# Two paddings in SBUF that move the stationary operands of the float32r matmuls

## The chip, the core and the metric

One core of one Trainium2 chip runs the whole kernel. The metric is the device time of one execution in microseconds; the median of several runs is given. The names of the engines are those of the profile: PE is TensorE, PEld its weight loads, DVE VectorE, ACT ScalarE, POOL GpSimd, SP SyncE, which issues nearly all DMAs.

## The reference

A transformer block over S = 2048 tokens of width D = 448, with 16 heads of 28 columns, and an MLP whose hidden width is split into two halves of FH = 896. Everything is float32.

```python
mod = (silu(c) @ w_mod).reshape(1, 6, 1, -1)          # sa, ca, ga, sb, cb, gb
h = layernorm(x) * (1 + ca) + sa
q, k, v = split(h @ wqkv)                              # 16 heads
o = softmax(q @ k.T * 28 ** -0.5) @ v
x = x + ga * (o @ wo)
h = layernorm(x) * (1 + cb) + sb
z = gelu(h @ w_in)
z1, z2 = z[..., :896], layernorm(z[..., 896:])
g = w_sp @ z2 + b_sp[:, None]                          # mixes the tokens, 2048 x 2048
x = x + gb * ((z1 * g) @ w_out)
```

## The kernel before

**Precision.** Most matmuls are in float32r, and each float32 operand is split into a high and a low part, both float32r. A product then takes several matmuls (high x high, low x high, high x low) that accumulate in PSUM. Where the contraction is over 448 rows, the list STEPS (11 pairs of a slice of the activations and a slice of the weights) says which parts meet. P·V and the transposes are in plain float32.

**Operands.** In `pe.matmul(out, a, b)`, `a` is the stationary operand, which a weight load puts into the array, at most 128 columns of 4 bytes, that is 512 bytes of each partition; `b` is the moving operand, 448 or 512 columns here. The profile names the moving operand first or last without meaning; what is stationary is told below.

**Memory.** Three pools last long: `const` at the low end of SBUF, `dpool` at the high end (side "right") with one big tile heapD, and pools that come and go between them. heapD is reused all through by views: hT (the normalised activations) and wqk (the weights of q and k), then OT (the output of attention) and wos, then w2 and half of z2, then uT. After attention three more big tiles come at the low end: heapA (w1, then part of z2), heapB (h2T, then the rest of z2 and the high part of w_out) and heapC (the last group of h2T, then the low part of w_out). Every view's slices are multiples of 448 or 512 elements apart, so all stationary slices taken from one big tile have the same first byte modulo 512.

**Stages, in order.**
- 0 to about 115 us: modulation vectors, layernorm, `ln_transpose`, `v_tile` (stationary hT in heapD, moving wv, L241) and `qk_unit` (stationary wqk, moving hT, both heapD, L249). The results of qk_unit go to DRAM (qk_scr) as a high and a low part.
- about 115 to 905 us: attention. For each head `load_head` brings k and q to `kst` and `qst`, three tiles of each in turn, in the pool `stk`. `m_mm` (L346: stationary qst, moving kst, 84 rows) makes scores whose row maxima DVE takes (L351, TENSOR_REDUCE); `m_fin` writes the negated maxima into two more rows of qst. `s_mm` (L377: stationary kst, moving qst, 86 rows) makes the scores less their maxima, of which ACT takes the exponential into P (L381). `pv_mm` (L392: stationary V, moving P, float32) follows for two units of 128 keys at a time. The order is written out by hand in the loop over `u` (256 units): four s_mm and four m_mm alternate, m_mm LEAD = 20 units ahead, and after each second unit 16 records of P·V. So a pair of units is a burst of 16 matmuls and then P·V. The PSUM tiles of both kinds come from one ring of seven. The last 20 units have s_mm alone.
- about 905 to 1010 us: `wo_mm` (stationary OT, moving wos, both heapD, L561), the second layernorm, `z1_unit` (stationary w1 in heapA, moving h2T in heapB or heapC, L672).
- to about 1097 us: `z2_gemm` (stationary h2T in heapB or heapC, moving w2 in heapD, L744) and `z2_norm`, which puts z2[0..7] in heapD, z2[8..11] in heapA and z2[12..15] in heapB.
- to the end: the mixing of tokens. For each block `tb` of 512 tokens, `mix_part(tb, st, f)` (L792, L793, L794: stationary z2[st], moving the high and low parts of the weights in `wsp`) runs over 16 values of st and 7 of f. `gate` forms u, split into uT (heapD), and `y_part` (stationary uT, moving w_out in heapB and heapC, L832 to L834) of one block is spread through the mixing of the next.

Tiles in a pool are laid out in the order in which they are asked for, so a tile that nothing uses moves those that come after it, and one in a pool on the right side moves all that lies below it.

Of the kernel before, what the change touches and what calls it, by code (L numbers as in the profile page):

```python
# [8 lines left out]
F32 = mybir.dt.float32  # L9
# [24 lines left out]
def tile_adaln_mha_gmlp(ctx, tc, x, wqkv, wo, w_in, w_spT, b_sp, w_out, cT, w_mod, out):  # L34
# [5 lines left out]
    dpool = ctx.enter_context(tc.tile_pool(name="dpool", bufs=1, side="right"))  # L40
# [17 lines left out]
        cols[nm] = const.tile([128, 4], F32, name=f"col_{nm}")  # L58
    bcs = {"gb": const.tile([128, D], F32, name="bc_gb")}

    heapD = dpool.tile([128, 24 * 896], F32R, name="heapD")

    def hview(heap, off, a, b):
        return heap[:, off : off + a * b].rearrange("p (a b) -> p a b", b=b)
# [254 lines left out]

    stk = att.enter_context(tc.tile_pool(name="stk", bufs=1))  # L320
    ppool = att.enter_context(tc.tile_pool(name="ppool", bufs=6))
    kst = [stk.tile([128, S], F32R, name=f"kst{i}") for i in range(3)]
    qst = [stk.tile([128, S], F32R, name=f"qst{i}") for i in range(3)]
    npool = att.enter_context(tc.tile_pool(name="npool", bufs=2))
# [584 lines left out]
```

## Time and profile before

| | |
|---|---|
| median of 3 runs | 1481.84 us (1479.3 to 1483.68) |
| the profiled execution | 1484.28 us |
| its span, first to last instruction | 1482.5 us |
| mean granted TensorE clock | 0.994 |
| DVE busy | 60% |
| ACT busy | 49% |
| POOL busy | 20% |

In a group's row, the tiles are out<-in, then rows x columns; after the first bar stand busy time in us and the mean duration of one in ns, after the second the idle time of the engine before them. Matmuls overlap in the pipeline, so a duration is longer than the distance between two starts; that distance is read from the first column of the timeline. A row of the timeline with x6 merges six neighbours: start of the first, time from there to the end of the last.

The first bytes of the stationary operands modulo 512, from the built program:

| stationary | lines | before |
|---|---|---|
| heapD: hT, wqk, OT, z2[0..7], uT | 241, 249, 561, 792 to 794, 832 to 834 | 480 |
| kst, qst | 346, 377 | 320 |
| heapA, heapB, heapC: w1, h2T, z2[8..15] | 672, 744, 792 to 794 | 64 |

### The profile page before, as it was taken

To read this page: it belongs to the slowest core of one execution; us is meant where nothing else is said; L and a number is where in the kernel's file an instruction comes from. 1 tells how busy PE (TensorE), PEld (TensorE's weight loads), DVE (VectorE), ACT (ScalarE), POOL (GpSimd) and SP (SyncE) were. 2 spreads that over 40 slices of the span, in tenths; PEclk is the share of its full clock that TensorE was granted. 3 is DMA by queue.
4 is the path that set the end of the run, shared out by engine and by line. 5 is a ranking of instruction groups with operands and counts; after the bars stand their busy time and mean duration, and the time that the engine had idled before them with its cause. 6 is when DMAs were issued, how large, how long until landed. Compare 5 with 4: busy or idle time off the path is not lost. (4 is left out here: it accounts for less than half of the span.)

```text
span 1482.5 us, 19584 instructions
## 1 busy us (share of the span) xinstructions
PE 1444.3 (97%) x7284; PEld 1014.8 (68%) x7284; DVE 891.8 (60%) x1469; ACT 723.7 (49%) x1374; POOL 294.2 (20%) x282
## 2 busy tenths in 40 slices
PE   4998999999999999999999999999999999999999
PEld 3886755555555555555555547778988888888887
DVE  6726888888888888888888821752541411413114
ACT  3522467677677676776776784343432210211111
POOL 4723300000002011101000021540763300302002
PEclk8999999999999999999999999999999999999999
DMA  9336402210122112221022004632003322323223
GB/s 233 107 108 203 151 17 52 52 41 25 40 52 52 39 35 57 52 48 43 16 51 52 12 20 122 206 111 100 8 21 102 114 75 68 106 62 101 84 68 106
DMA packets 58790, 111.57 MB, mean 75 GB/s; under 512 B 12006, under 2 KB 27462, under 8 KB 56006
## 3 DMA queue, kind: packets, MB, share of 16 engines
q1 hardware_dynamic: 58534, 109.40, 25.9%
q8 instruction: 57, 0.93, 0.3%
q0 software_dynamic: 160, 0.92, 0.2%
q14 instruction: 39, 0.32, 0.1%
HBM read 76.15 MB, written 29.49 MB: 71 GB/s over the span
## 5 line engine op out<-in xcount | busy, mean ns | idle before, releaser
L351 DVE TENSOR_REDUCE pm<-mt 128x1 f32<-128x512 f32 x1024 | 628.1, 682 | 131.0 <-PE mt L346 129.8
L381 ACT ACTIVATE P<-st_ps 128x512 f32<-128x512 f32 x1024 | 514.2, 620 | 153.7 <-PE st_ps L377 153.3
L377 PE MATMUL st_ps<-qst,kst 86*128 86x512 f32 x1024 | 409.8, 411 | 0.0
L346 PE MATMUL mt<-kst,qst 84*128 84x512 f32 x1024 | 400.7, 397 | 5.2 <-DMA qst<-qk_scr 3.2
L377 PEld LDWEIGHTS st_ps<-qst,kst 86*128 86x128 f32 x1024 | 192.8, 189 | 145.1 <-issue 80.5
L392 PE MATMUL o_ps<-P,V 128*32 128x512 f32 x2048 | 247.5, 598 | 0.0
L346 PEld LDWEIGHTS mt<-kst,qst 84*128 84x128 f32 x1024 | 194.6, 190 | 45.0 <-DVE pm L351 4.5
L70 DVE TENSOR_TENSOR wsp_l<-raw_sp,wsp_h 128x512 fp32r<-128x512 f32 x64 | 48.7, 763 | 193.0 <-ACT wsp_h L727 193.0
L727 ACT ACTIVATE wsp_h<-raw_sp 128x512 fp32r<-128x512 f32 x64 | 40.4, 631 | 248.6 <-DMA raw_sp<-in_w_spT_dram 170.9
L392 PEld LDWEIGHTS o_ps<-P,V 128*32 128x32 f32 x2048 | 54.1, 109 | 123.1 <-issue 116.2
L70 POOL TENSOR_TENSOR heapD<-u,heapD 128x512 fp32r<-128x512 f32 x27 | 44.6, 1685 | 261.2 <-ACT heapD L811 261.2
L418 POOL TENSOR_TENSOR osb<-osb,rb 128x512 f32<-128x512 f32 x16 | 20.4, 1277 | 366.3 <-DMA rb<-r_scr 220.7
L792 PE MATMUL acc<-wsp_h,heapD 128*128 128x512 f32 x224 | 89.2, 398 | 2.9 <-ACT zg L747 1.6
L794 PE MATMUL acc<-wsp_h,heapD 128*128 128x512 f32 x224 | 88.5, 395 | 0.0
L793 PE MATMUL acc<-wsp_l,heapD 128*128 128x512 f32 x224 | 88.3, 394 | 0.0
L249 PE MATMUL pq<-heapD 128*128 128x512 f32 x308 | 79.8, 398 | 0.0
L249 PEld LDWEIGHTS pq<-heapD 128*128 128x128 f32 x308 | 58.6, 191 | 13.6 <-issue 0.4
L70 POOL TENSOR_TENSOR nl<-nf,nh 16x128 fp32r<-16x128 f32 x16 | 7.2, 451 | 272.8 <-issue 180.6
L672 PE MATMUL z_ps<-heapB,heapA 128*128 128x512 f32 x231 | 54.5, 396 | 0.0
L744 PE MATMUL z_ps<-heapD,heapB 128*128 128x448 f32 x264 | 53.0, 363 | 0.0
L837 DVE TENSOR_TENSOR x2t<-x2t,y_ps 128x448 f32<-128x448 f32 x12 | 7.5, 621 | 75.7 <-PE y_ps L834 75.7
L744 PEld LDWEIGHTS z_ps<-heapD,heapB 128*128 128x128 f32 x264 | 49.6, 188 | 3.3
(156 smaller groups left out, 1629.0 us busy)
## 6 DMA issues: line engine op xcount, KB each, us to landing
raw_sp<-in_w_spT_dram SPq DMA_DIRECT2D x64, 256.0 KB
kst<-qk_scr SPq DMA_DIRECT2D x48, 224.0 KB
qst<-qk_scr SPq DMA_DIRECT2D x48, 224.0 KB
qk_scr<-qh SPq DMA_DIRECT2D x28, 256.0 KB
qk_scr<-ql SPq DMA_DIRECT2D x28, 256.0 KB
z_scr<-z1t SPq DMA_DIRECT2D x28, 256.0 KB
z<-z_scr SPq DMA_DIRECT2D x28, 256.0 KB
wm<-in_w_mod_dram SPq DMA_DIRECT2D x6, 784.0 KB
```

The source lines that it names most:

```text
L70: eng.tensor_tensor(out=dst, in0=a, in1=hi.bitcast(F32), op=ALU.subtract)
L249: pe.matmul(pq, wqk[:, b, m * 128 : (m + 1) * 128], hT[g][:, a, :], start=j == 0, stop=j == NST - 1)
L346: pe.matmul(mt, qst[h % 3][0:84, t * 128 : (t + 1) * 128], kst[h % 3][0:84, kb * 512 : (kb + 1) * 512], start=True, stop=True)
L351: dve.tensor_reduce(out=pms[h][:, t, kb : kb + 1], in_=mt, axis=AX.X, op=ALU.max)
L377: pe.matmul(st, kst[h % 3][0:86, kt * 128 : (kt + 1) * 128], qst[h % 3][0:86, qb * 512 : (qb + 1) * 512], start=True, stop=True)
L381: act.activation(p, st, AF.Exp, scale=SCALE)
L392: pe.matmul(otile[h][32 * qb : 32 * qb + 32, :], V[:, kt, h, :], ptiles.pop((u, qb)), start=kt == 0, stop=kt == NT - 1)
L672: pe.matmul(ps_t, w1[:, b, f * 128 : (f + 1) * 128], h2T[g][:, a, :], start=j == 0, stop=j == NST - 1)
L744: pe.matmul(ps_t[:, :D], h2T[g][:, a, tt * 128 : (tt + 1) * 128], w2[:, b, hf * D : (hf + 1) * D], start=j == 0, stop=j == NST - 1)
L792: pe.matmul(acc[f], z2[st][:, 0, fs], hi, start=st == 0, stop=False)
L793: pe.matmul(acc[f], z2[st][:, 0, fs], lo, start=False, stop=False)
L794: pe.matmul(acc[f], z2[st][:, 1, fs], hi, start=False, stop=st == NT - 1)
```

## The change

A tile of 104 float32 per partition is asked for behind heapD, in the pool on the right side, and one of 64 float32 ahead of kst and qst. Neither is read or written. heapD and what lies below it on the right side (the staging tiles of q, k and of the heads' outputs) move down by 416 bytes, so that heapD starts at 64 modulo 512; kst, qst and what follows them in `stk` and the pools after it (the P buffers, the small tiles of the maxima) move up by 256 bytes, so that kst and qst start at 64 modulo 512. heapA, heapB, heapC, V and wsp stay. The moving operands in the moved tiles move with them: wqk's partner hT, kst and qst, P, wos, and w2, whose first bytes go from 480 and 224 to 64 and 320.

```diff
@@ -58,7 +58,9 @@
         cols[nm] = const.tile([128, 4], F32, name=f"col_{nm}")
     bcs = {"gb": const.tile([128, D], F32, name="bc_gb")}
 
+
     heapD = dpool.tile([128, 24 * 896], F32R, name="heapD")
+    dpool.tile([128, 104], F32, name="padD")
 
     def hview(heap, off, a, b):
@@ -319,6 +321,7 @@
 
     stk = att.enter_context(tc.tile_pool(name="stk", bufs=1))
     ppool = att.enter_context(tc.tile_pool(name="ppool", bufs=6))
+    stk.tile([128, 64], F32, name="padS")
     kst = [stk.tile([128, S], F32R, name=f"kst{i}") for i in range(3)]
     qst = [stk.tile([128, S], F32R, name=f"qst{i}") for i in range(3)]
```

## The prediction, made before the run

> **What bounds the kernel now.** I read the page first, for the share of each engine by slice; then the groups of instructions with shapes kept apart, for the same matmul from different tiles; then the timeline, for the distance between neighbouring starts; last the built program's addresses, since the change moves nothing else.
>
> ```profile
> span 1482.5 us, 19584 instructions
> PE 1444.3 (97%) x7284; PEld 1014.8 (68%) x7284; DVE 891.8 (60%) x1469; ACT 723.7 (49%) x1374; POOL 294.2 (20%) x282
> ```
>
> TensorE is busy 97% of the span, so what counts is the distance from one matmul start to the next. The diff can act on nothing else: in the built program every instruction, operand shape and wait stands where it stood, on all five engines. Only addresses differ. heapD moves from byte 143328 to 142912 (480 to 64 modulo 512), kst and qst move up by 256 bytes (320 to 64), and with them the P buffers and the staging tiles. So no wait is added or moved past.
>
> The trace of before already holds the comparison. In the mixing stage `z2[st]` lies in heapD for st 0 to 7 (480), in heapA and heapB for st 8 to 15 (64); the moving `wsp` tiles are at 64 throughout, and code, stage and shapes are one. Groups, last figures before the second bar: busy us, mean ns of one:
>
> ```profile
> L792 PE MATMUL acc<-wsp_h,heapD 128*128 128x512 f32 x224 | 89.2, 398 | 2.9 <-ACT zg L747 1.6 <-DVE u L809 1.3
> L793 PE MATMUL acc<-wsp_l,heapD 128*128 128x512 f32 x224 | 88.3, 394 | 0.0
> L794 PE MATMUL acc<-wsp_h,heapD 128*128 128x512 f32 x224 | 88.5, 395 | 0.0
> L792 PE MATMUL acc<-wsp_h,heapA 128*128 128x512 f32 x112 | 43.6, 390 | 0.0
> L793 PE MATMUL acc<-wsp_l,heapB 128*128 128x512 f32 x112 | 43.6, 390 | 0.0
> L833 PE MATMUL y_ps<-heapB,heapD 128*128 128x448 f32 x98 | 36.1, 368 | 0.0
> L744 PE MATMUL z_ps<-heapD,heapC 128*128 128x448 f32 x88 | 17.8, 362 | 0.0
> ```
>
> The heapD groups average 396 ns, those from heapA and heapB 390. L744, 448 columns and a stationary at 64, takes 362 to 363; L833, 448 columns and a stationary in heapD, 368. The timeline (start, duration) says that this is real spacing and no matter of how an end is modelled:
>
> ```profile
> 1199.70 0.40 PE L792 MATMUL acc<-wsp_h,heapD 128*128 128x512 f32 x1
> ...
> 1201.10 0.40 PE L792 MATMUL acc<-wsp_h,heapD 128*128 128x512 f32 x1
> 1224.84 0.39 PE L792 MATMUL acc<-wsp_h,heapA 128*128 128x512 f32 x1
> ...
> 1226.20 0.39 PE L792 MATMUL acc<-wsp_h,heapA 128*128 128x512 f32 x1
> ```
>
> Each pair is six matmuls apart: 1.40 us, 233 ns each, from heapD; 1.36 us, 227 ns each, from heapA.
>
> The Trainium skill speaks against the change here: "TensorE: Matmul & The Clock Gate", on step 1 of what a matmul does, says that TensorE reads stationary and moving operands through two independent SBUF ports, so that a weight load takes nothing from the running matmul. By that rule no address could matter. The 233 against 227 ns with one moving operand disagrees with it.
>
> **The change part by part.** Where the stationary lies in heapD and TensorE sets the pace:
> 1. Mixing from heapD, 3 x 224 = 672 matmuls, whose operands become 64 and 64 as those from heapA are now: (396 - 390) x 672, with unrounded means 5.7 ns, gives 3.8 us. Waits there are 2.9 us of 270, so nearly all is path.
> 2. y_part, 336 matmuls of 448 columns: 368 or 367 down to 363, 4.8 ns each, 1.6 us. It runs between the mixing matmuls, on the path.
> 3. v_tile, 176: six in the timeline take 1.39 us where six of L744 take 1.36, 5 ns apart once last durations are taken off; 0.9 us, 0 if the first 100 us (TensorE idle in places) swallow it.
> 4. wo_mm, 176: spacing 202 to 207 ns against L744's 200, 2.5 ns at least, 0.4 us (1.2 at most).
> 5. qk_unit, 308: stationary and moving are both at 480. Six in a row, from 102.69 us, take 1.52 us with the last one's 0.39, or 226 ns apart: nothing to gain. Between attention's matmuls they run slower, for the reason under attention. 0.
> 6. z2_gemm, 352, stationary unmoved at 64; its moving operand goes from 480/224 to 64/320. Now exactly 200 ns. No row has 448 columns with both at 64/320. Bounds: 0, and the 2.5 to 6.7 ns by which wo_mm (both operands in heapD, equal offsets) exceeds 200, a loss of 0.9 to 2.3 us. I take 0, since every group with a stationary at 64 is at its floor whatever it streams.
>
> **Attention** (L346, L377: 2048 matmuls, mean spacing 234 ns) would be the largest prize: 7 ns x 1888 (16 in each of the 118 pairs of units that hold both kinds) is 13 us. I take 0. Its stationary sits at 320, and at 320 it already runs at the low spacing once the two kinds stop alternating:
>
> ```profile
> 599.29 0.40 PE L346 MATMUL mt<-kst,qst 84*128 84x512 f32 x1
> ...
> 600.71 0.40 PE L346 MATMUL mt<-kst,qst 84*128 84x512 f32 x1
> 889.42 2.10 PE L377 MATMUL st_ps<-qst,kst 86*128 86x512 f32 x8
> ```
>
> Alternating 84 and 86 rows: six starts in 1.42 us, 237 ns. In the tail, eight score matmuls alone: 2.10 less the first gap of 0.34 and the last duration of 0.39, over six, is 228 ns, and the last two gaps are 226 and 227. The weight load tells the same: 190 ns after a matmul with another row count (L346's row has 190), 187 to 188 after one with the same. So the row count breaks the rhythm there, not the address. The bound above 0: a burst of 16 between two P·V groups could shorten by some 100 ns. But the weight load of its 15th matmul waits for the fourth reduction (L351, every 598 ns in the burst): in some 3 bursts of 10 it starts 106 ns or less before its matmul, and there an earlier PE only waits longer. So 0.7 x 100 + 0.3 x 25 = 78 ns, times 118 = 9 us. VectorE is next: eight reductions need 4.8 of a pair's 5.8 us.
>
> Weight loads of P·V (V unmoved, P moving) and the transposes show no dependence on offset: 0, as are the staging tiles' DMAs, which land behind a busy TensorE.
>
> **Sum.** 3.8 + 1.6 + 0.9 + 0.4 = 6.7 us. The profiled execution took 1484.28 us (span 1482.5 and 1.8 outside): 1477.6. It stands 2.4 us above the median of 1481.84, so 1475.1 in terms of medians, which I forecast.
>
> **The rivals** (median terms).
> - Attention gains as well: the pad was put there on the view that 320 is as bad as 480, and 234 ns equals heapD's 233. For it speaks that equality; against it the tail. 6.7 + 9 = 15.7: 1466.1; with no wait for the reductions, 1462.
> - Only the difference between the two operands' offsets counts. qk_unit at 480/480 and 226 ns speaks for it, z2_gemm's 200 at two differences against. Then mixing still gains 3.8, y_part, v_tile and wo_mm nothing, z2_gemm loses up to 2.3: 1478.0 to 1480.3.
> - Nothing happens: heapD may be slow for its place (above byte 142900, the others below 126100) and not its offset. qk_unit's 226 ns from heapD speaks against. 1481.8. The Trainium skill, "SBUF — State Buffer", Operand start alignment, asks only that an operand start at a multiple of its element size, which both layouts satisfy; it speaks of legality and not speed, and no run here bears on it otherwise.
> - Slower: attention settles at a worse rhythm. L377 to L346 shows gaps of 240 within bursts. If 240 became the rule in place of 233.3, 6.7 x 1888 = 12.6 us less the gain of 6.7: 1487.7. It decides from 6.7 / 1888 = 3.5 ns a matmul. Against it: the offset that goes away, 320, and the new one have nothing in the trace that tells them apart.
>
> **How the numbers follow.** Forecast 0.46; attention too 0.20; difference only 0.14; nothing 0.08; slower 0.12. A measurement of this kernel tells 0.3%, 4.4 us, from no change. The forecast (6.7) lies beyond that, with some chance of falling short of it: faster 0.66, same 0.21, slower 0.13. The likeliest case alone spans 1473 to 1478. The range reaches from attention's gain at 1463 to 1485, leaving out the rest of the slower case.
>
> **What would show it.** Right: heapD groups of L792 to L794 at 390, y_part's at 363, L744 still 362 to 363, L346 still about 397 with spacing 234 in attention. Wrong: L744 up at 365 to 369 (difference rules); L346 and L377 spaced 227 (attention gains), with longer waits of the L377 weight loads for L351; heapD still at 396 (place rules).

## The result and the profile after

| | before | after |
|---|---|---|
| median | 1481.76 us (20 runs) | 1476.2 us (20 runs) |
| ratio | | 0.9968, 95% interval 0.9957 to 0.998 |
| a second series, medians | 1480.91 us (20 runs) | 1475.71 us (8 runs) |
| ratio | | 0.9967, 0.9956 to 0.9978 |
| the profiled execution | 1484.28 us, span 1482.5 | 1473.13 us, span 1471.4 |

In the first series one execution of each kernel took far longer than the rest (2026.81 and 2867.84 us); the ratios leave such executions out. The kernel is 5.6 us faster by the first medians and 5.2 by the second. The two profiled executions lie 11.1 us apart, so one must not put the whole of that down to the change; the table of stages below separates it.

The page after, engines' busy time and share of the span:

```profile
span 1471.4 us, 19584 instructions
PE 1439.4 (98%) x7284; PEld 1015.8 (69%) x7284; DVE 888.1 (60%) x1469; ACT 723.4 (49%) x1374; POOL 294.6 (20%) x282
```

TensorE still bounds the kernel. The lines of the changed file are 2 or 3 higher: L795 to L797 are mix_part, L835 to L837 y_part, L747 z2_gemm, L349 and L380 m_mm and s_mm. The groups of instructions after, shapes kept apart (after the first bar: busy us, mean ns):

```profile
L795 PE MATMUL acc<-wsp_h,heapD 128*128 128x512 f32 x224 | 87.8, 392 | 1.9 <-ACT zg L750 1.2 <-DVE u L812 0.7
L796 PE MATMUL acc<-wsp_l,heapD 128*128 128x512 f32 x224 | 87.4, 390 | 0.1
L797 PE MATMUL acc<-wsp_h,heapD 128*128 128x512 f32 x224 | 87.4, 390 | 0.0
L795 PE MATMUL acc<-wsp_h,heapA 128*128 128x512 f32 x112 | 43.7, 390 | 0.0
L835 PE MATMUL y_ps<-heapB,heapD 128*128 128x448 f32 x98 | 35.7, 365 | 0.0
L836 PE MATMUL y_ps<-heapB,heapD 128*128 128x448 f32 x98 | 36.0, 367 | 0.0
L747 PE MATMUL z_ps<-heapD,heapC 128*128 128x448 f32 x88 | 18.0, 366 | 0.0
L349 PE MATMUL mt<-kst,qst 84*128 84x512 f32 x1024 | 401.3, 397 | 5.5 <-DMA qst<-qk_scr 3.5 <-DVE pm L354 1.6 <-ACT P L384 0.3
```

The mixing matmuls from heapD fell from 394 to 398 ns to 390 to 392, where those from heapA were all along. y_part went from 367 or 368 to 364 to 367, and not to 363. z2_gemm, whose stationary did not move, went up from 362 to 366. m_mm is where it was, at 397. The timeline of the mixing says the same in spacing: six starts in 1.36 us, 227 ns each, with stationary operands from heapD.

```profile
1194.68 0.39 PE L795 MATMUL acc<-wsp_h,heapD 128*128 128x512 f32 x1
...
1196.04 0.39 PE L795 MATMUL acc<-wsp_h,heapD 128*128 128x512 f32 x1
```

From the start records of both traces I took, for each function, the mean distance from one matmul to the next, leaving out distances over 260 ns, which are waits:

| function (columns) | before, ns | after, ns | count | gain, us |
|---|---|---|---|---|
| mix_part, heapD (512) | 233.4 | 227.5 | 672 | 4.0 |
| y_part (448) | 205.2 | 202.4 | 335 | 0.9 |
| v_tile (448) | 205.9 | 202.6 | 176 | 0.6 |
| wo_mm (448) | 203.1 | 203.5 | 176 | -0.1 |
| z2_gemm (448) | 200.1 | 202.7 | 352 | -0.9 |
| qk_unit (512) | 230.4 | 229.6 | 308 | 0.2 |
| m_mm, s_mm in bursts (512) | 234.3 | 234.2 | 1968 | 0 to 0.2 |

The last row counts 1024 s_mm, with those of the tail, and 944 m_mm. Together that makes 4.7 us, close to the 5.2 and 5.6 of the medians. By stages, each counted from the first matmul of one function to the first of the next:

| stage, us | before | after | after, second series |
|---|---|---|---|
| v_tile to s_mm | 154.6 | 150.8 | 150.4 |
| s_mm to wo_mm (attention) | 728.0 | 728.1 | 728.1 |
| wo_mm to z1_unit | 42.0 | 41.9 | 41.6 |
| z1_unit to z2_gemm | 78.4 | 76.8 | 77.5 |
| z2_gemm to mix_part | 72.2 | 72.7 | 72.7 |
| mix_part to the end | 384.8 | 379.1 | 380.5 |

Attention did not move at all, z2_gemm's stage got longer, mixing shorter by 4.3 to 5.7 us. The first stage looks 4 us shorter, but that is mostly how executions differ: in the runs below it lasts between 150.4 and 154.5 us whatever heapD's offset (150.9 and 151.2 with heapD at 480, 154.5 in one with heapD at 64).

### The profile page after: what moved, and what is told of

Its sections match the earlier page's. It is cut to its first block, busy times and chain, and to the rows that moved or that the text cites. A ratio compares the mean times of both kernels' runs of the same rounds, so it can differ in the third digit from the quotient of the medians.

```text
span 1471.4 us, 19584 instructions
## 1 busy us (share of the span) xinstructions
PE 1439.4 (98%) x7284; PEld 1015.8 (69%) x7284; DVE 888.1 (60%) x1469; ACT 723.4 (49%) x1374; POOL 294.6 (20%) x282
## 5 line engine op out<-in xcount | busy, mean ns | idle before, releaser
L380 PE MATMUL st_ps<-qst,kst 86*128 86x512 f32 x1024 | 410.1, 411 | 0.0
L349 PE MATMUL mt<-kst,qst 84*128 84x512 f32 x1024 | 401.3, 397 | 5.5 <-DMA qst<-qk_scr 3.5
L380 PEld LDWEIGHTS st_ps<-qst,kst 86*128 86x128 f32 x1024 | 192.9, 189 | 144.8 <-issue 80.5
L349 PEld LDWEIGHTS mt<-kst,qst 84*128 84x128 f32 x1024 | 195.3, 191 | 45.6 <-DVE pm L354 4.5
L795 PE MATMUL acc<-wsp_h,heapD 128*128 128x512 f32 x224 | 87.8, 392 | 1.9 <-ACT zg L750 1.2
L797 PE MATMUL acc<-wsp_h,heapD 128*128 128x512 f32 x224 | 87.4, 390 | 0.0
L747 PE MATMUL z_ps<-heapD,heapB 128*128 128x448 f32 x264 | 53.7, 366 | 0.0
L747 PEld LDWEIGHTS z_ps<-heapD,heapB 128*128 128x128 f32 x264 | 49.7, 188 | 3.9
```

Source lines behind the costliest of these rows:

```text
L349: pe.matmul(mt, qst[h % 3][0:84, t * 128 : (t + 1) * 128], kst[h % 3][0:84, kb * 512 : (kb + 1) * 512], start=True, stop=True)
L380: pe.matmul(st, kst[h % 3][0:86, kt * 128 : (kt + 1) * 128], qst[h % 3][0:86, qb * 512 : (qb + 1) * 512], start=True, stop=True)
L747: pe.matmul(ps_t[:, :D], h2T[g][:, a, tt * 128 : (tt + 1) * 128], w2[:, b, hf * D : (hf + 1) * D], start=j == 0, stop=j == NST - 1)
L795: pe.matmul(acc[f], z2[st][:, 0, fs], hi, start=st == 0, stop=False)
L797: pe.matmul(acc[f], z2[st][:, 1, fs], hi, start=False, stop=st == NT - 1)
```

## The experiments

Two things were open. First, whether the stationary operand's own offset counts, as the change's words have it, or the difference between the moving operand's and the stationary's. z2_gemm's loss spoke for the second. Second, whether attention's 234 ns comes from its row counts. A difference below is always moving less stationary, modulo 256.

**Each padding alone.**

```diff
 # e1: the changed kernel
-    stk.tile([128, 64], F32, name="padS")
 # e2: the changed kernel
-    dpool.tile([128, 104], F32, name="padD")
```

> The change with padD alone; kst and qst stay at 320. Theory (attention's pace comes from its alternating row counts, 84 and 86, and heapD's offset is all that works): same as with both paddings, 4 to 6 us below the kernel before; mixing matmuls from heapD 390 to 392 ns, attention spaced 234 ns. Rival (kst and qst at 64 give part of the gain): 2 us or more slower than with both.

> The change with padS alone; heapD stays at 480. Theory: within 1.5 us of the kernel before, attention spaced 234 ns, mixing from heapD still 396 ns. Rival (kst and qst at 64 give part of the gain): 2 to 9 us below the kernel before, with attention's spacing under 234.

Measured: padD alone 1478.46 us against 1480.4 of the kernel before, ratio 0.9981 (0.9969 to 0.9994); padS alone 1482.07, ratio 1.001 (0.9998 to 1.0022). The time with padD alone came out less far below before than expected (1.9 us and not 4 to 6); its interval overlaps that of both paddings, so the times by themselves do not exclude the rival. The traces decide it. One group of mixing from heapD, first with padD alone, then with padS alone:

```profile
L796 PE MATMUL acc<-wsp_h,heapD 128*128 128x512 f32 x224 | 87.3, 390 | 0.0
```

```profile
L796 PE MATMUL acc<-wsp_h,heapD 128*128 128x512 f32 x224 | 88.9, 397 | 0.0
```

With padD alone the mixing from heapD is spaced 227.4 ns, y_part 202.4, z2_gemm 202.7 and attention takes 727.6 us, each as with both. With padS alone mixing stays at 233.3, z2_gemm at 200.1, and attention takes 727.4. kst and qst at 64 in place of 320 do nothing.

**The stationary stays at 480, the moving operand goes there.** This is the kernel before, without either padding, and with one in front of the mixing weights:

```diff
     wp = ctx.enter_context(tc.tile_pool(name="wp", bufs=2))
+    wp.tile([128, 104], F32, name="padW", bufs=1)
```

> The kernel before, with the moving tiles wsp of the mixing 416 bytes further on: from 64 to 480 modulo 512. heapD, and with it half of the stationary z2, stays at 480. Theory (the difference of moving and stationary counts, modulo 256): heapD's mixing now has difference 0 and goes from 233.4 to 227.5 ns; heapA and heapB get 416, which is 160 modulo 256, as z2_gemm before, and stay at 227; 4 us below the kernel before. Rival (the stationary's own offset counts, 480 is bad and 64 good): heapD stays at 233 and heapA, heapB at 227, the time within 1.5 us of before.

Measured: 1482.31 us, ratio 1.0008 (1.0 to 1.0017). The groups of this run:

```profile
L793 PE MATMUL acc<-wsp_h,heapD 128*128 128x512 f32 x224 | 87.6, 391 | 2.2 <-ACT zg L748 1.6 <-DVE u L810 0.6
L795 PE MATMUL acc<-wsp_h,heapD 128*128 128x512 f32 x224 | 87.2, 389 | 0.0
L793 PE MATMUL acc<-wsp_h,heapA 128*128 128x512 f32 x112 | 44.4, 396 | 0.0
L795 PE MATMUL acc<-wsp_h,heapB 128*128 128x512 f32 x112 | 44.4, 396 | 0.0
```

The two have changed places. From heapD, still at 480, the matmuls are now spaced 227.4 ns; from heapA and heapB, still at 64, 234.1 and 234.2. So 480 is not a bad offset and 64 not a good one; what counts is the difference, and 0 is the best of those tried for 512 columns. I had expected heapA and heapB to stay at 227, since their difference became 160, at which z2_gemm ran at its best; that half was wrong. A difference of 160 suits z2_gemm's 448 columns and not these 512. The total is the same as before because 672 matmuls gained what 672 others lost.

**Other differences.** Four runs of the changed kernel with other offsets (the lines that these replace, and the enlarged tiles, are left out):

```diff
 # e4: heapD holds 8 float32 more, padD 8 fewer; moving operands 32 bytes on
+    wos = hview(heapD, 14344, 8, D)
+    w2 = hview(heapD, 14344, 8, 896)
+    wouts_h = hview(heapB, 7176, 7, D)
+    wouts_l = hview(heapC[0], 8, 7, D)
+    wv = hview(wvt, 8, 8, D)
 # e6: in the same places, w2 16, w_out's parts 32, wos 48, wv 56 float32 on
 # e9 and e10: heapD at 320, heapD at 192
-    dpool.tile([128, 104], F32, name="padD")
+    dpool.tile([128, 40], F32, name="padD")   # e9; 72 in e10
```

> The changed kernel, with the moving operands of the 448-column matmuls (wv, wos, w2 and both parts of w_out) 32 bytes further on; the stationary operands stay at 64, so moving less stationary is 32 modulo 128, as it was in z2_gemm before. Theory (the difference of the two offsets counts): z2_gemm back from 202.7 to 200 ns, y_part from 202.4 to 200, v_tile and wo_mm from 203 to 200; 352 x 2.7 + 336 x 2.4 + 176 x 3 + 176 x 3.5 = 2.9 us below the changed kernel. Rival (the stationary's own offset counts, and the 202.7 has another cause): these groups stay at 202 to 203.5 and the time within 1 us.

> The changed kernel, with the moving operands of the four 448-column gemms moved by different amounts, the stationary ones left at 64: w2 by 64 bytes, w_out's parts by 128, wos by 192, wv by 224. A scan: spacing of z2_gemm, y_part, wo_mm, v_tile at differences 64, 128, 192 and 224 modulo 256. Known so far: 0 gives 202.4 to 203.5, 32 gives 205 to 206.7, 96 gives 205.2, 160 gives 200. Theory (the difference counts): at least two of the four leave 202 to 203.5 by more than 2 ns. Rival (the stationary's own offset counts, the rest is chance): all four within 2 ns of 202.7.

> The changed kernel with the padding behind heapD cut from 104 to 40 float32, so that heapD starts at 320 modulo 512 in place of 64: against wsp the difference is 256, which is 0 modulo 256. Theory (the difference counts modulo 256): heapD's mixing at 227.5 ns, z2_gemm 202.7, y_part 202.4, all as in the changed kernel. Rival (modulo 512, as the change's words have it): heapD's mixing leaves 227.5 by more than 2 ns.

> The changed kernel with the padding behind heapD cut to 72 float32, so that heapD starts at 192: differences against wsp and w_out of -128, that is 128 modulo 256, and z2_gemm's of 128. Theory (modulo 256): 128 is neither 0, the good difference for 512 columns, nor 160, the best for 448; heapD's mixing at 229 to 234 ns, y_part at 203 as with difference 128 in the scan. Rival (modulo 128): as in the changed kernel, 227.5, 202.7 and 202.4.

Measured spacings, with the kernels before and after for comparison:

| difference modulo 256 | 512 columns (mix_part, heapD) | z2_gemm | y_part |
|---|---|---|---|
| 0 | 227.5 (after), 227.4 (e9) | 202.7 (after, e9) | 202.4 (after, e9) |
| 32 | | 206.7 (e4) | 205.5 (e4) |
| 64 | | 200.0 (e6) | |
| 96 | 233.4 (before) | | 205.2 (before) |
| 128 | 232.7 (e10) | 204.0 (e10) | 203.2 (e6), 204.2 (e10) |
| 160 | 234.2 (heapA, heapB in e5) | 200.1 (before) | 203.3 (e7, below) |

e4 missed: I took modulo 128 and expected 200, and z2_gemm went the other way, to 206.7. With y_part at 205.5, wo_mm at 205.1 and v_tile at 204.9 the four lost 1.4 + 1.0 + 0.3 + 0.4 = 3.1 us against the changed kernel, two thirds of its gain by spacing. The time, 1479.89 us, ratio 0.9995 (0.9983 to 1.0008), can't be told from the kernel before. Two of its groups:

```profile
L748 PE MATMUL z_ps<-heapD,heapC 128*128 128x448 f32 x88 | 18.3, 369 | 0.0
L837 PE MATMUL y_ps<-heapB,heapD 128*128 128x448 f32 x98 | 36.1, 368 | 0.0
```

The scan e6 came out between its two expectations: z2_gemm alone lies more than 2 ns from 202.7, where the first asked for two of the four outside their band and the second for none (wo_mm at 192 had 202.3, v_tile at 224 had 204.1). Its time was 1476.73 us, ratio 0.9969 (0.9957 to 0.9981). e9, with heapD at 320, is like the changed kernel in the spacings of mix_part, z2_gemm and y_part and in time (three executions), 1476.89 us, ratio 0.9971 (0.9955 to 0.9988): modulo 512 is not needed, modulo 256 is enough. z2_gemm says the same within one trace: its two halves have differences 256 bytes apart, and both run at 200 ns before (200.2 and 200.0) and at 202.6 and 202.7 after. e10, at 192, loses the mixing's gain (232.7 ns) and has 1480.03 us, ratio 0.9998 (0.9988 to 1.0009): modulo 128 is not enough. One group of mixing from heapD, first of e9, then of e10:

```profile
L797 PE MATMUL acc<-wsp_h,heapD 128*128 128x512 f32 x224 | 87.3, 390 | 0.0
```

```profile
L797 PE MATMUL acc<-wsp_h,heapD 128*128 128x512 f32 x224 | 88.4, 395 | 0.0
```

Two limits of the table: the 64 was tried with z2_gemm alone, and at 160 y_part does not follow z2_gemm.

**Equal row counts in attention.** The changed kernel, with the maxima's matmul over 86 rows; the two rows of qst that it now reads as well are set to zero, so that they add nothing:

```diff
-    stk.tile([128, 64], F32, name="padS")
+    zrow = stk.tile([128, 64], F32, name="padS")
+    pool.memset(zrow, 0.0)
 # in load_head
+        sp.dma_start(
+            q[84:86, :].bitcast(F32).rearrange("p (a b) -> p a b", b=64), zrow[0:2, None, :].broadcast_to([2, 32, 64])
+        )
 # in m_mm
-        mt, qst[h % 3][0:84, t * 128 : (t + 1) * 128], kst[h % 3][0:84, kb * 512 : (kb + 1) * 512], start=True, stop=True
+        mt, qst[h % 3][0:86, t * 128 : (t + 1) * 128], kst[h % 3][0:86, kb * 512 : (kb + 1) * 512], start=True, stop=True
```

> The changed kernel, and the maxima's matmul reads 86 rows of qst and kst as the scores' does; the two added rows of qst are set to zero by a DMA of 16 KB per head before. Theory (a weight load after a matmul with another row count takes 190 ns in place of 188, and that holds the spacing at 234): weight loads at 188 ns, spacing in attention's bursts falling from 234 to 227 to 230 within a burst, 70 to 100 ns less per pair of units, 6 to 12 us less in all than the changed kernel, less what the wait for the reductions takes back. Rival (the alternation of two tiles, or VectorE at work beside, sets the 234): spacing stays 233 to 234 and the time within 2 us of the changed kernel.

Measured: 1474.15 us against 1480.4 of the kernel before, ratio 0.9952 (0.9933 to 0.9971). Weight loads of the changed kernel first, then of this run:

```profile
L349 PEld LDWEIGHTS mt<-kst,qst 84*128 84x128 f32 x1024 | 195.3, 191 | 45.6 <-DVE pm L354 4.5 <-issue 3.9 <-ACT P L384 2.1
L380 PEld LDWEIGHTS st_ps<-qst,kst 86*128 86x128 f32 x1024 | 192.9, 189 | 144.8 <-issue 80.5 <-DVE pm L354 16.2 <-ACT P L384 9.0
```

```profile
L353 PEld LDWEIGHTS mt<-kst,qst 86*128 86x128 f32 x1024 | 192.8, 188 | 41.1 <-issue 4.8 <-DVE pm L358 4.0 <-ACT P L388 2.1
L384 PEld LDWEIGHTS st_ps<-qst,kst 86*128 86x128 f32 x1024 | 191.1, 187 | 150.4 <-issue 80.5 <-DVE pm L358 17.0 <-ACT P L388 12.7
```

The maxima's load has two more rows, and yet takes 188 ns in place of 191; the scores' load, with its 86 rows unchanged, takes a median of 190 ns behind one of 84 rows and 188 behind one of 86. The timeline of one of its bursts, in the middle and at the end:

```profile
601.99 0.39 PE L353 MATMUL mt<-kst,qst 86*128 86x512 f32 x1
...
603.35 0.39 PE L353 MATMUL mt<-kst,qst 86*128 86x512 f32 x1
603.58 0.40 PE L384 MATMUL st_ps<-qst,kst 86*128 86x512 f32 x1
603.81 0.40 PE L353 MATMUL mt<-kst,qst 86*128 86x512 f32 x1
604.05 0.40 PE L384 MATMUL st_ps<-qst,kst 86*128 86x512 f32 x1
```

Six starts in 1.36 us, 227 ns each, in a stage where the two kinds still alternate and VectorE still works beside; then 230 to 240 ns at the end of the burst. Over the 116 bursts of 16 that the trace holds whole, the median distances from the second matmul on are 236, 229, 232, 231, then 227 six times, then 230, 233, 239, 234. The first four are a run-in: the distances after a P·V group, before the rhythm is steady. The last four are where the 13th and 15th weight loads wait for the reductions (the DVE releaser in the rows above). In the median burst the 15th starts 176 ns ahead of its matmul, where the changed kernel has 210: still in time, but the rhythm of 227 is broken at that end of the burst. By means over all bursts, the first eleven distances together are 52 ns shorter than in the changed kernel and the last four 9 ns longer. Attention took 723.3 us in place of 728.1, 4.8 less, below the 6 to 12 expected: that wait and the run-in after each P·V group keep the rest. The run excludes the alternation by itself and VectorE's work beside as the cause of the 234. It doesn't tell whether the change of row count slows the matmuls or the 84 rows as such, since it removes both.

**Attention with a difference of 128.** The run with equal rows once more, with a padding of 32 float32 between kst and qst:

> The run with equal rows, and qst 128 bytes further on than kst, so that the difference is 128 modulo 256 in both kinds of attention's matmuls where it was 0. Theory (the difference counts): the run-in after P.V, 236, 229, 232, 231 ns before 227 is reached, changes, to all 227 if 128 is a good difference (attention 0 to 2 us shorter than with equal rows, the wait for the reductions taking the rest) or to 233 to 240 if it is a bad one (2 to 9 us longer). Rival (the difference doesn't count in attention): the same run-in and the same time within 1 us.

Measured: 1472.69 us, ratio 0.9943 (0.9926 to 0.996). The run-in changed: the median distances are 234, 230, 232, 229, 232, then 230 five times, then 233, 234, 233, 236; 227 is not reached. So moving qst and what lies behind it does act here, while attention's time is the same, 723.6 us: by means, the first eleven distances are 14 ns longer than with equal rows alone and the last four, where the wait for the reductions had made them long, 9 ns shorter.

The run hides a second question. The load that runs beside a matmul is the next one's, as the timeline of this run shows:

```profile
601.22 0.39 PE L385 MATMUL st_ps<-qst,kst 86*128 86x512 f32 x1
601.22 0.19 PEld L354 LDWEIGHTS mt<-kst,qst 86*128 86x128 f32 x1
```

s_mm streams qst while qst is loaded for m_mm, and m_mm streams kst while kst is loaded for s_mm. So in a burst the difference between the two tiles that are read at the same time stayed 0, and only that between a matmul's own operands became 128. In the tail, where s_mm follows s_mm, both became 128: there the last five median distances are 241, 233, 231, 231, 229, where equal rows alone have 228, 233, 231, 226, 227, and mixing at 128 (e10) has stretches of 241, 233, 231, 231, 229 as well. In the functions of the table above the two differences are the same, so which of them counts stays open.

The 1.5 us between this run's median and that of e3 come from two different series and are inside the intervals.

**Versions put together.** Both take equal rows and move the 448-column gemms' operands by 160 bytes; e11 leaves w_out where it was. The diff shows the moved operands alone:

```diff
+    wos = hview(heapD, 14336 + 40, 8, D)
+    w2 = hview(heapD, 14336 + 40, 8, 896)
+    wv = hview(wvt, 40, 8, D)
+    wouts_h = hview(heapB, 7168 + 40, 7, D)     # e7 alone
+    wouts_l = hview(heapC[0], 40, 7, D)         # e7 alone
```

> Candidate for a faster version: the changed kernel, the moving operands of all four 448-column gemms 160 bytes further on, so that the difference is 160 modulo 256 as it was in z2_gemm before; and the maxima's matmul with 86 rows (the added ones zero) as in the run with equal rows. Theory: z2_gemm, y_part, v_tile, wo_mm all at 200 ns, 0.9 + 0.8 + 0.5 + 0.6 = 2.8 us, and attention as with equal rows, 4.4 us shorter: 6 to 8 us below the changed kernel, 10 to 12 below the kernel before. Rival (z2_gemm's 200 was owed to its own tiles): only z2_gemm returns to 200, 5 us below the changed kernel.

> The candidate without the shift of w_out: the changed kernel, w2, wos and wv 160 bytes further on, w_out where it was, and the maxima's matmul with 86 rows. Theory: z2_gemm 200, wo_mm and v_tile 201, y_part 202.4, attention 4.4 us shorter: 4.4 + 0.9 + 0.4 + 0.2 = 5.9 us below the changed kernel run beside it. Rival (the wait for the reductions takes attention's gain back): 1 to 2 us below it.

> The changed kernel once more, for comparison in the same series: 0.996 to 0.998 of the kernel before, mixing from heapD 227.5 ns, attention 234 ns, z2_gemm 202.7 ns. A rival that the earlier 5.6 us were in part the state of the chip would have it at 0.998 to 1.0.

Measured: e7 1475.24 us against 1481.7 of the kernel before, ratio 0.9951 (0.9937 to 0.9965): 6.5 us less, where 10 to 12 were expected. z2_gemm 200.1, wo_mm 201.0 and v_tile 201.2 ns came about as expected, so the 200 is not z2_gemm's alone; y_part did not (203.3, up from 202.4). y_part runs in groups of 6 or 9 between mixing matmuls, so it never has long enough at one rhythm; that this is the cause was not tried. The changed kernel run again came as expected, ratio 0.9967, with mixing from heapD at 227.4 ns, attention at 234 and z2_gemm at 202.7. e11 1473.67 us, ratio 0.9955 (0.9943 to 0.9967), beside the changed kernel's 1475.71: 2.0 us by medians, with overlapping intervals, where 5.9 were expected. Its v_tile came to 202.8 ns and wo_mm to 201.7 (201 expected). In its trace attention is 3.9 us shorter (724.2) and z2_gemm's stage 0.5 (72.2), as the theory has it and not the rival, whose time fits; but the stage of wo_mm lasts 43.5 us and not 41.6, and the first one 152.6 and not 150.4. In all runs the first varies by 4 us and wo_mm's is near either 42 or 44, in e1 too, which shares nothing of this with e11, so I do not put it down to the edit, nor can I exclude the added DMAs at the start. A gain over the changed kernel is shown for attention, not for the whole kernel beyond its uncertainty.

## Why the prediction was right, and where its steps were off

The time came within 1.1 us of the forecast, and its largest term held. The mechanism did not hold as the prediction had it, that a group with a stationary operand at 64 is at its floor whatever it streams: what counts is the difference between the two operands. The number is right all the same because heapD's mixing, the term that carries it, gains under both accounts: the change gives it the operands of heapA, at 64 and 64. That the times came out nearer to the forecast than the spacings did (5.6 and 5.2 us against 4.7) is luck, within the interval of 3.0 to 6.4 us that the first ratio gives. One of the prediction's own signs of being wrong appeared: L744, now L747, is up at 366 ns, in the 365 to 369 that stood for "difference rules".

- **No instruction and no wait moved, only addresses; TensorE's spacing is all that can change.** Held: the same 19584 instructions, and the waits' rows of TensorE are alike (m_mm 5.2 us idle before, 5.5 after).
- **Mixing from heapD, 3.8 us.** 233.4 to 227.5 ns over 672 matmuls is 4.0. The comparison inside the trace of before gave the size.
- **Attention, 0 against a prize of 13 us.** Held: with padS alone nothing happens, and with equal row counts the spacing in the burst's middle falls from 234 to 227. The bound from the wait for the reductions held as well: equal rows brought 4.8 us, where the prediction had worked out 9 for a gain in attention and 13 without that wait. It counted a cost only where the load comes too late; the last four distances of the bursts show one where it is merely later than usual. Its reading of the weight loads, 190 ns after another row count and 187 to 188 after the same, fits the bursts and the tail but not the stage of qk_unit: there, in the trace of before, the 40 loads of 84 rows that follow one of 128 rows take a median of 188 ns, and the 40 that follow one of 84 take 190. So that the longer load is what slows the matmuls is not shown.
- **y_part 1.6, v_tile 0.9, wo_mm 0.4.** Measured 0.9, 0.6 and none. These terms took z2_gemm's 200 ns as the floor that a stationary at 64 gives. With a difference of 0 the 448-column matmuls go to 202.4 to 203.5 and no lower.
- **z2_gemm 0, with a bound of 0.9 to 2.3 us lost.** It lost 0.9. The value that I took rested on one sentence, that every group with a stationary at 64 is at its floor whatever it streams. The run with wsp at 480 refutes it: stationary at 64, and 234 ns.
- **The second rival, only the difference counts, 0.14.** It had the mechanism. I held z2_gemm's 200 ns "at two differences" against it, but 480 and 224 less 64 are 416 and 160, which are one and the same modulo 256. Its price was wrong too: it had y_part and v_tile gaining nothing, though their differences went from 96 to 0, and so ended at 1478.0 to 1480.3, too high.
- **The sum.** 6.7 us forecast; 4.7 by the spacings, 5.6 and 5.2 by the medians. The mis-sized terms are those of the 448-column matmuls: 2.9 us in the sum, 0.5 measured (y_part, v_tile and wo_mm gave 1.4, z2_gemm took 0.9). Mixing and qk_unit brought 0.2 each more than their terms.
- **Place rather than offset.** Refuted: heapD reaches 227 ns at 64 and 320, in the upper part of SBUF, and at 480 too with wsp moved; heapA loses it without having moved.

The Trainium skill's rule, in "TensorE: Matmul & The Clock Gate", step 1 of what a matmul does, is that loading the next weights takes no read bandwidth from the running matmul, since the two operands are read through independent ports. For the time of these float32r matmuls that is not the whole of it: one and the same matmul takes 227 or 234 ns by how the two operands' addresses differ. What in the array or the memory makes them depend on each other is not shown by any run here, nor that it is bandwidth; nor why 448 columns do best at other differences (z2_gemm at 64 and 160) than 512, of which 0, 96, 128 and 160 were tried.

## What to carry to other kernels

Where TensorE is busy all the time, compare the spacing of like matmuls that take their operands from different tiles; a steady 3% between them is worth finding. Before padding a tile, change the offset of the other operand as well: only the run that moved the moving operand told that the difference matters and not an alignment, and a pad that helps one matmul moves the operands of others too. Where two kinds of matmul alternate with different numbers of rows, it is worth trying rows of zeros to make them equal; here it shortened attention by 4.8 us of 728.

## What was not expected of the hardware

- The spacing of these float32r matmuls depends on the first bytes of the two operands, moving less stationary, modulo 256. For 512 columns it is 227 ns at 0 and 233 to 234 at 96, 128 and 160. For 448 columns it is 200 in z2_gemm at 64 and 160, 202 to 204 at 0 and 128, 205 to 207 at 32 and 96; y_part at 160 has 203 and not 200.
- After a P·V group the spacing, at a difference of 0, needs some five matmuls to settle (236, 229, 232, 231, 227 ns). Where matmuls of 84 and 86 rows alternate it does not settle there: 233 to 234 ns throughout.
- In attention, a weight load of 86 rows takes a median of 190 ns behind one of 84 rows and 188 behind one of 86.
